# A second layer of 512 rows in seven block products, with its weight scale from squares

## The chip, the cores and the metric

The kernel runs on one core of a Trainium2 chip. The metric is device time in microseconds (us). Before the change the median of three runs is 934.13 us (931.35 to 936.52).

## The reference

Three parts follow one another: a decayed linear attention (4 x 8 heads of 768 steps, 48 wide), a gated dense mixture on its 3072 x 384 output, and a second mixture with eight experts, of which each token takes the best two:

```python
for e in range(E):                       # 8 experts
    for k in range(2):
        mask = top2[:, k] == e
        h = np.maximum(x[mask] @ w1[e], 0.0)                # 384 -> 1024
        out[mask] += top2_w[mask, k, None] * (h @ w2[e])    # 1024 -> 384
```

## The kernel before

Everything in float32 is carried as two float16 halves, high and low; a product A x B is three matmuls, high x high, high x low, low x high, added up in PSUM. `split` cuts a tile: ScalarE copies it to float16 (line 180), VectorE subtracts that copy from it (line 182 or 184).

The change lies in the second mixture (`experts`, line 1107). Each expert has 832 slots for its tokens: part 0 of 512 rows, part 1 of 320, the last 64 of which (`first_few`, `last_few`) are computed only if the expert has more than 768 tokens, inside a branch on the chip. The tokens are gathered by GpSimd's indirect DMAs and turned by SP's transposing DMAs.

- First layer (`layer1`): for each of eight blocks of 128 hidden units, 9 matmuls of 512 or 256 columns fill one PSUM bank (there are eight); ScalarE takes the relu as high half, VectorE relu minus high half as low half.
- Second layer (`layer2`): for each tile of 128 rows, 24 matmuls of 384 columns, hidden blocks as stationary operand; ScalarE scales the result by each row's gate (`put`) and GpSimd adds it to the output in memory by an indirect DMA.
- Weights of the expert after next (`weight_steps`) are fetched in halves on SP's queue into three float32 buffers, `greatest` finds the largest magnitude, `over_all` spreads it over partitions by a one-column matmul, `scales` makes powers of two of it, `cut_up` splits. These steps stand in the list `todo`, and `prepare(n)` issues the next n of them, behind the last VectorE and ScalarE instruction issued so far.

The order of an expert e is: first layer of part 0 (eight blocks, in the first two of which the short rest of expert e-1 is finished), the short rest's first layer, first layer of part 1, four second-layer tiles of part 0, two of part 1. TensorE's order is as written; each engine works through its instructions in one fixed order.

Of the kernel before, what the change touches and what calls it, by code (L numbers as in the profile page):

```python
# [78 lines left out]


@with_exitstack
def body(ctx, tc, q, k, v, alpha, mw1, mw2, mw3, mwo, wg, wn, noise, ew1, ew2, out, dbg=None):
# [39 lines left out]
    wp = ph1.enter_context(tc.tile_pool(name="wp", bufs=1))  # L122
    xp = ph1.enter_context(tc.tile_pool(name="xp", bufs=3))
    sp = ph1.enter_context(tc.tile_pool(name="sp", bufs=2))
    gp = ph1.enter_context(tc.tile_pool(name="gp", bufs=2))
    ps = ph1.enter_context(tc.tile_pool(name="ps1", bufs=8, space=PSUM))
# [711 lines left out]
    ep = None  # L838
# [26 lines left out]
    def weight_steps(src, e, n, m, hi, lo, sc):  # L865
# [25 lines left out]
        def scales():  # L891

            nc.vector.tensor_copy(sc[:, 1:2], s["pm"])
            nc.vector.tensor_scalar(sci[:, 2:3], sci[:, 1:2], 0x7F800000, None, op0=OP.bitwise_and)
            nc.vector.tensor_scalar(sci[:, 2:3], sci[:, 2:3], float(64 << 23), None, op0=OP.max)
            nc.vector.tensor_scalar(sci[:, 3:4], sci[:, 2:3], -1.0, float(258 << 23), op0=OP.mult, op1=OP.add)
            nc.vector.tensor_scalar(sci[:, 4:5], sci[:, 2:3], -float(4 << 23), None, op0=OP.add)
# [5 lines left out]

        return ([lambda i=i: get(i) for i in range(2)] + [lambda i=i: greatest(i) for i in range(2)] +
# [48 lines left out]
    def put(py, n, mt, wv, t, e=None):  # L953
        ys = ep.tile([P, DM], F32, name="ysb", bufs=3)
        nc.scalar.activation(ys[:n], py, AF.Copy, scale=wv[:n, t:t + 1])  # L955

        def add():
# [25 lines left out]
    EW, EX, EH, WV = {}, {}, {}, {}  # L983
# [60 lines left out]

    def second(e, p, t, midway=None):
# [45 lines left out]

    def next_weights(e):
        a, b = weights_for(e)
        todo.extend(pause(1) + a[2:4] + pause(1) + a[5:10] + b[1:2] + a[10:] + pause(1) + b[2:4] + pause(2) + b[5:])
# [12 lines left out]
    def experts():  # L1107
# [5 lines left out]
        rank(NG - 1)  # L1113
        rb = ep.tile([P, E], BF, name="rb", bufs=1)
# [30 lines left out]
        for e in range(1, E):  # L1145
            if e > 1:
                for f in range(NF):
                    first(e, 0, f)
# [24 lines left out]
            for t in range(NTP[0]):  # L1173
                second(e, 0, t)
                prepare(2)
                if e + 1 < E:
                    turn_part(e + 1, 0, t)
            prepare(len(todo))
            if e + 2 < E:
                next_weights(e + 2)  # L1180
            if e < E - 1:
                for t in range(NTP[1] - 1):
                    turn_part(e + 1, 1, t)
                    py = cleared(NK) if t else None
                    second(e, 1, t)
                turn_part(e + 1, 1, NTP[1] - 1)
# [4 lines left out]
        return li  # L1191

# [103 lines left out]
    overflow(li)  # L1296
    ph1.close()
# [31 lines left out]
```

## Time and profile before

| what | value |
|---|---|
| median of 3 runs | 934.13 us |
| profiled execution | 934.74 us, span 933.0 us |
| TensorE busy | 898.9 us, 96% |
| VectorE, ScalarE, GpSimd busy | 67%, 48%, 28% |
| granted TensorE clock, mean | 0.986 |

The span is the profiled execution without what lies around it (1.74 us). Matmuls overlap, so their pace is read from the distance of their starts and not from a row's length. The profile calls TensorE PE (its weight loads PEld), VectorE DVE, ScalarE ACT, GpSimd POOL and SyncE SP.

### The profile page before, as it was taken

What the parts mean: (1) busy time and instruction counts of PE and PEld (TensorE: products, weight loads), DVE (VectorE), ACT (ScalarE), POOL (GpSimd) and SP (SyncE); (2) the same over time, 40 slices, a digit from 0 to 9 for tenths busy, and PEclk for the clock granted to TensorE, in tenths of its full rate; (3) what the DMA queues carried; (4) which work ended last, traced back from release to release, by engine and by line L of the source; (5) the groups of instructions that cost most, each with busy time, mean ns of one, the idle gap of its engine ahead of it and who ended that gap; (6) DMA issues with size and microseconds to landing.
All of it is one profiled execution on the core that took longest, in us unless ns stands there. A gap on an engine that the chain in (4) does not pass through costs nothing. (4 is left out here: it accounts for less than half of the span.)

```text
span 933.0 us, 17675 instructions
## 1 busy us (share of the span) xinstructions
PE 898.9 (96%) x6824; PEld 600.8 (64%) x6824; DVE 624.3 (67%) x1733; ACT 448.2 (48%) x916; POOL 258.3 (28%) x246
## 2 busy tenths in 40 slices
PE   8779999999999999999999999999999999999997
PEld 4667777777767666576665555865656565657574
DVE  7998878488779789597768874556455555555320
ACT  2576766364475654755546534334343443434321
POOL 2311110003041131514132234442333333343203
PEclk9889899999999999999999999999999999999999
DMA  9889582241504435101129248495768677776304
GB/s 244 230 150 148 143 199 76 35 94 49 122 10 104 68 95 77 44 26 42 63 69 195 94 77 205 79 221 95 190 118 182 130 163 148 154 156 137 39 10 48
DMA packets 189274, 105.63 MB, mean 113 GB/s; under 512 B 156912, under 2 KB 174912, under 8 KB 189184
## 3 DMA queue, kind: packets, MB, share of 16 engines
q1 hardware_dynamic: 172624, 68.04, 33.8%
q0 software_dynamic: 16560, 36.37, 18.2%
q8 instruction: 59, 0.97, 0.4%
q14 instruction: 31, 0.25, 0.1%
HBM read 73.06 MB, written 20.31 MB: 100 GB/s over the span
## 5 line engine op out<-in xcount | busy, mean ns | idle before, releaser
L958 POOL DMA_INDIRECT out_dram<-ysb,mt x56 | 88.3, 1578 | 145.0 <-ACT ysb L955 138.0
L922 PE MATMUL ps<-xT,eh 128*128 128x256 f16 (+1 forms) x384 | 125.0, 326 | 1.8 <-DVE hl L926 0.6
L934 PE MATMUL ps<-eh,hl 128*128 128x384 f16 x384 | 125.2, 326 | 0.0
L933 PE MATMUL ps<-el,hh 128*128 128x384 f16 x384 | 125.2, 326 | 0.0
L932 PE MATMUL ps<-eh,hh 128*128 128x384 f16 x384 | 125.1, 326 | 0.0
L924 PE MATMUL ps<-xT,el 128*128 128x256 f16 (+1 forms) x384 | 125.1, 326 | 0.0
L923 PE MATMUL ps<-xT,eh 128*128 128x256 f16 (+1 forms) x384 | 125.1, 326 | 0.0
L926 DVE SCALAR_TENSOR_TENSOR hl<-ps,hh 128x512 f16<-128x512 f32 (+1 forms) x128 | 69.6, 554 | 79.4 <-ACT hh L925 75.3
L925 ACT ACTIVATE hh<-ps 128x512 f16<-128x512 f32 (+1 forms) x128 | 62.3, 489 | 79.5 <-PE ps L924 65.9
L955 ACT ACTIVATE ysb<-ps,wv 128x384 f32<-128x384 f32 (+1 forms) x56 | 32.4, 579 | 136.5 <-PE ps L934 67.9
L700 POOL DMA_INDIRECT table<-md,ad x48 | 51.3, 1069 | 155.4 <-DVE ad L697 103.7
L184 DVE SCALAR_TENSOR_TENSOR el<-es,esc,eh 128x512 f16<-128x512 f32 (+1 forms) x80 | 66.9, 853 | 35.2 <-ACT eh L180 34.9
L545 ACT ACTIVATE ab<-ps 128x384 f32<-128x384 f32 (+2 forms) x136 | 63.1, 471 | 39.4 <-PE ps L543 24.1
L910 POOL DMA_INDIRECT xg<-x2s,mt x56 | 54.4, 971 | 99.7 <-DMA mt<-table 64.7
L182 POOL TENSOR_TENSOR sm<-sf,sm 128x512 f16<-128x512 f32 x24 | 30.0, 1278 | 153.9 <-ACT sm L180 153.9
L541 PE MATMUL ps<-xT,w0h 128*128 128x384 f16 (+2 forms) x204 | 65.0, 320 | 0.9 <-ACT xT L408 0.9
L541 PE MATMUL ps<-xT,w1h 128*128 128x384 f16 (+2 forms) x204 | 65.1, 320 | 0.8 <-DVE Kt L246 0.4
L570 PE MATMUL ps<-Wh,gh 128*128 128x400 f16 x192 | 63.9, 333 | 1.8 <-ACT gh L180 1.5
L542 PE MATMUL ps<-xT,w1h 128*128 128x384 f16 (+2 forms) x204 | 65.1, 320 | 0.0
L543 PE MATMUL ps<-xT,w0l 128*128 128x384 f16 (+2 forms) x204 | 65.0, 320 | 0.0
L542 PE MATMUL ps<-xT,w0h 128*128 128x384 f16 (+2 forms) x204 | 65.0, 320 | 0.0
L543 PE MATMUL ps<-xT,w1l 128*128 128x384 f16 (+2 forms) x204 | 65.0, 319 | 0.0
(303 smaller groups left out, 2085.5 us busy)
## 6 DMA issues: line engine op xcount, KB each, us to landing
es<-in_moe_w_dram SPq DMA_DIRECT2D x32, 768.0 KB
s<-in_moe_w_dram POOLq DMA_DIRECT2D x16, 512.0 KB
out_dram<-zero POOLq DMA_DIRECT2D x5, 960.0 KB
v<-in_v_dram SPq DMA_DIRECT2D x24, 192.0 KB
x2s<-xr SPq DMA_DIRECT2D x24, 192.0 KB
pad<-in_alpha_dram SPq DMA_DIRECT2D x21, 192.0 KB
pad<-in_q_dram SPq DMA_DIRECT2D x21, 192.0 KB
pad<-in_k_dram SPq DMA_DIRECT2D x21, 192.0 KB
```

Source lines behind the costliest of these rows:

```text
L184: nc.vector.scalar_tensor_tensor(lo, src, scale, hi, op0=OP.mult, op1=OP.subtract)
L541: nc.tensor.matmul(pm, wab[i][0][:, kk, fs], xT[:, kk, cs], start=kk == 0, stop=False)
L542: nc.tensor.matmul(pm, wab[i][0][:, kk, fs], xT[:, NK + kk, cs], start=False, stop=False)
L543: nc.tensor.matmul(pm, wab[i][1][:, kk, fs], xT[:, kk, cs], start=False, stop=kk == NK - 1)
L922: nc.tensor.matmul(pm, w1h[:, kk, fs], xT[:, kk, :n], start=kk == 0, stop=False)
L923: nc.tensor.matmul(pm, w1h[:, kk, fs], xT[:, NK + kk, :n], start=False, stop=False)
L924: nc.tensor.matmul(pm, w1l[:, kk, fs], xT[:, kk, :n], start=False, stop=kk == NK - 1)
L926: nc.vector.scalar_tensor_tensor(hl[:, f], pm, 0.0, hh[:, f], op0=OP.max, op1=OP.subtract)
L932: nc.tensor.matmul(py[:n], hh[:, f, ts], w2h[:, f], start=f == 0, stop=False)
L933: nc.tensor.matmul(py[:n], hh[:, f, ts], w2l[:, f], start=False, stop=False)
L934: nc.tensor.matmul(py[:n], hl[:, f, ts], w2h[:, f], start=False, stop=f == NF - 1)
L958: i = nc.gpsimd.indirect_dma_start(out=out, out_offset=bass.IndirectOffsetOnAxis(ap=mt[:n, t, 0:1].bitcast(U32), axis=0), in_=ys[:n], in_o ...
```

## The change

For experts 2 to 7 the second layer of part 0, (512 x 1024) x (1024 x 384), is cut into 2 x 2 blocks (256 rows, 512 hidden units, 192 columns) and done in seven block products, in Winograd's form of Strassen's scheme. Left operands are blocks of the hidden tile, or sums of them; right operands are blocks of the second weights, or differences of them.

- `first_pair` replaces `first` there: blocks come in pairs (f, f + 4), and after the second of a pair VectorE forms four sums, and six of the seven left operands are split from float32.
- The weight list of these experts grows by `diffs` and four `pairs`: four differences of weight blocks and their halves.
- `second_pair` does the products for two tiles of 128 rows each; some products add into a bank that has been read before. Results are scaled into `yq` by ScalarE, or scaled and added by VectorE; four sends go out in the last two products.
- For all experts `greatest` is a square with a running sum on ScalarE, written over the place of the high half, and `scales` works from the mean square.
- The order of the weight steps is new: two steps after each product and after each second-layer tile of part 1, the first fetch after the third product, the next two after the last.

```diff
         def greatest(i):
-            nc.vector.tensor_reduce(sc[:, 5 + i:6 + i], s[i], AX.XY, OP.max, apply_absolute_value=True)
+            nc.scalar.activation(half(hi, i), s[i], AF.Square, accum_out=sc[:, 5 + i:6 + i])
             if i:
                 s["m"] = ep.tile([P, 1], BF, name="em")
-                nc.vector.tensor_reduce(s["m"], sc[:, 5:7], AX.X, OP.max)
+                nc.vector.tensor_tensor(s["m"], sc[:, 5:6], sc[:, 6:7], OP.add)
...
+        def differ(x):
+
+            t = s["d", x] = qp.tile([P, HT, HD], F32, name="td", bufs=3)
+            a, b = ((block(0, 1), block(0, 0)), (block(1, 1), s.get(("d", 0))),
+                    (block(1, 0), s.get(("d", 1))), (block(0, 1), block(1, 1)))[x]
+            nc.vector.tensor_tensor(t, a, b, OP.subtract)
+
+        def cut_diff(x):
+            split(s["d", x], ET[e][0][:, x], ET[e][1][:, x], sc[:, 3:4])
+
+        def diffs():
+
+            ET[e] = [qp.tile([P, 4, HT, HD], F16, name=f"t{y}") for y in "hl"]
+            differ(0)
+            differ(1)
+
+        def pairs(x):
+            cut_diff(x)
+            if x < 2:
+                differ(x + 2)
...
+    def first_pair(e, i):
+
+        f = i // 2 + i % 2 * HT
...
+        if i % 2 == 0:
+            u = qp.tile([P, 6, HP], F32, name="u", bufs=3)
+            nc.scalar.activation(u[:, 0], pm[:, 0], AF.Relu)
+            V.scalar_tensor_tensor(u[:, 5], pm[:, 1], 0.0, u[:, 0], op0=OP.max, op1=OP.subtract)
+            EH[e, "u"] = (u, pm)
+            return
+        u, p0 = EH.pop((e, "u"))
+        nc.scalar.activation(u[:, 1], pm[:, 1], AF.Relu)
+        V.scalar_tensor_tensor(u[:, 2], p0[:, 1], 0.0, u[:, 1], op0=OP.max, op1=OP.add)
+        V.tensor_tensor(u[:, 3], u[:, 2], u[:, 0], OP.subtract)
+        V.scalar_tensor_tensor(u[:, 4], pm[:, 0], 0.0, u[:, 3], op0=OP.max, op1=OP.subtract)
+        nc.scalar.activation(bh[:, 2, j], pm[:, 0], AF.Relu)
+        V.scalar_tensor_tensor(bl[:, 2, j], pm[:, 0], 0.0, bh[:, 2, j], op0=OP.max, op1=OP.subtract)
+        split(u[:, :4], ah[:, :, j], al[:, :, j])
+        split(u[:, 4:], bh[:, :2, j], bl[:, :2, j])
...
+        sums = ((X, 0, plain(0, 0)), (Z, 6, plain(1, 0)), (X, 3, diff(1)), (Y, 2, diff(0)), (X, 5, diff(3)),
+                (Y, 4, plain(1, 1)), (X, 1, diff(2)))
+        after = ((0, 0, False), (0, 0, True), (0, 1, False), (1, 1, False), (1, 1, True), (0, 1, True), (1, 0, False))
+        for m, ((bk, x, (rh, rl)), (r, c, add)) in enumerate(zip(sums, after)):
+            lh, ll = left(x)
+            for k in range(n):
...
+                for f in range(HT):
+                    nc.tensor.matmul(bk[k], lh[:, f, ts], rh[:, f], start=new and f == 0, stop=False,
+                                     skip_group_check=True)
+                    nc.tensor.matmul(bk[k], lh[:, f, ts], rl[:, f], start=False, stop=False, skip_group_check=True)
+                    nc.tensor.matmul(bk[k], ll[:, f, ts], rh[:, f], start=False, stop=f == HT - 1,
+                                     skip_group_check=True)
...
+                if add:
+                    nc.vector.scalar_tensor_tensor(o, bk[k], wv[:, t:t + 1], o, op0=OP.mult, op1=OP.add)
+                else:
+                    nc.scalar.activation(o, bk[k], AF.Copy, scale=wv[:, t:t + 1])
+                if m >= len(sums) - 2:
+                    send(ys[k][r], P, mt, t, e)
+            between(m)
...
+    def next_pair(e, a, b):
+        a[1]()
+        b[0]()
+        todo.extend(a[2:3] + pause(3) + a[3:4] + pause(1) + a[5:10] + b[1:2] + a[10:] + b[2:3] + pause(5) +
+                    b[3:4] + pause(1) + b[5:])
...
+    def between(e, m):
+        prepare(2)
+        if m == 2 and e + 2 < E:
+            EW["next"] = open_weights(e + 2)
+        if e + 1 < E and 2 <= m < 2 + NTP[0]:
+            turn_part(e + 1, 0, m - 2)
```

## Rows read from the trace of the kernel before

**Rows 1.** The page's first part: engine, busy us, share of the span, instructions.

```profile
PE 898.9 (96%) x6824; PEld 600.8 (64%) x6824; DVE 624.3 (67%) x1733; ACT 448.2 (48%) x916; POOL 258.3 (28%) x246
```

**Rows 2.** Windows: start:end and length, then busy us of each engine, clock, DMA.

```profile
500.00:550.00 50.00, 48.16 (x274) 25.89 (x273) 43.67 (x165) 27.20 (x56) 7.50 (x8) 1.00 0.52 114
679.00:727.00 48.00, 47.70 (x296) 28.41 (x294) 25.93 (x47) 19.20 (x35) 17.55 (x14) 1.00 0.76 152
```

**Rows 3.** Waits of TensorE from 500 us on: total us, times, longest.

```profile
PE ps L889 <- DVE em L884: 1.1, 1, 1.1
```

**Rows 4.** Timeline of TensorE and its weight loads: start, us, engine, line, operation.

```profile
631.54 0.19 PE L946 MATMUL ps<-hh,eh 128*128 128x64 f16 x1
...
679.21 0.38 PE L922 MATMUL ps<-xT,eh 128*128 128x512 f16 x1
...
695.75 0.27 PE L922 MATMUL ps<-xT,eh 128*128 128x256 f16 x1
...
703.60 0.33 PE L932 MATMUL ps<-eh,hh 128*128 128x384 f16 x1
...
711.43 0.32 PE L932 MATMUL ps<-eh,hh 128*128 128x384 f16 x1
...
727.03 0.38 PE L922 MATMUL ps<-xT,eh 128*128 128x512 f16 x1
...
838.90 0.19 PE L1036 MATMUL ps<-xT,eh 128*128 128x64 f16 x1
...
919.71 0.19 PE L946 MATMUL ps<-hh,eh 128*128 128x64 f16 x1
919.71 0.10 PEld L947 LDWEIGHTS <-el 128*128 128x128 f16 x1
...
919.74 0.10 PEld L948 LDWEIGHTS <-eh 128*128 128x128 f16 x1
...
921.81 0.33 PE L932 MATMUL ps<-eh,hh 128*128 128x384 f16 x1
```

**Rows 5.** Timeline of VectorE in expert 2's first layers.

```profile
645.35 0.15 DVE L894 TENSOR_SCALAR esc<-esc 128x1 int32<-128x1 int32 x1
645.54 0.15 DVE L895 TENSOR_SCALAR esc<-esc 128x1 int32<-128x1 int32 x1
...
650.40 0.42 DVE L926 SCALAR_TENSOR_TENSOR hl<-ps,hh 128x256 f16<-128x256 f32 x1
650.73 0.75 DVE L184 SCALAR_TENSOR_TENSOR el<-es,esc,eh 128x512 f16<-128x512 f32 x1
```

**Rows 6.** Groups by line in 679 to 727 us, then two of the whole span.

```profile
L958 POOL DMA_INDIRECT out_dram<-ysb,mt x7 | 10.8, 1548 | 13.5 <-ACT ysb L955 13.2 <-issue 0.3
...
L881 DVE TENSOR_REDUCE esc<-es 128x1 f32<-128x1536 f32 x4 | 7.0, 1744 | 0.0
...
L926 DVE SCALAR_TENSOR_TENSOR hl<-ps,hh 128x512 f16<-128x512 f32 x8 | 5.5, 689 | 10.6 <-ACT hh L925 9.3 <-issue 1.3
...
L180 ACT ACTIVATE eh<-es,esc 128x768 f16<-128x768 f32 x4 | 3.5, 924 | 0.0
L955 ACT ACTIVATE ysb<-ps,wv 128x384 f32<-128x384 f32 x6 | 3.5, 581 | 16.9 <-issue 6.9 <-PE ps L934 6.1 <-PE ps L889 3.9
L926 DVE SCALAR_TENSOR_TENSOR hl<-ps,hh 128x256 f16<-128x256 f32 x8 | 3.3, 418 | 0.2 <-ACT hh L925 0.2
L925 ACT ACTIVATE hh<-ps 128x256 f16<-128x256 f32 x8 | 3.1, 385 | 1.5 <-PE ps L924 1.5
...
L182 DVE TENSOR_TENSOR gl<-ab,gh 128x384 f16<-128x384 f32 x60 | 34.0, 566 | 14.9 <-ACT gh L180 13.6 <-issue 1.2
L180 ACT ACTIVATE sm<-sf 128x512 f16<-128x512 f32 x24 | 14.9, 630 | 17.3 <-DVE sf L306 16.0 <-issue 1.1
```

**Rows 7.** Single lines: engine, operation, count, duration ns min/median/max.

```profile
L950 ACT ACTIVATE yt<-ps x8: 325/331/331, 597.4 to 922.0; 128x192 f32<-128x192 f32 x8
...
L575 ACT ACTIVATION_READ_ACCUMULATOR xr<-ps x24: 188/194/215, 173.6 to 528.9; 128x1 f32 x24
```

More of the change, by code (lines that the diff above doesn't have):

```diff
@@ L78 @@
 SX2 = SW * SW * SG * SW
+NQ = 2
+HP = G0 // 2
+HT = NF // 2
+HD = DM // 2
 @with_exitstack
@@ L121, in body @@
     ph1 = ExitStack()
[L122 to L123 removed]
+    ps = ph1.enter_context(tc.tile_pool(name="ps1", bufs=8, space=PSUM))
     sp = ph1.enter_context(tc.tile_pool(name="sp", bufs=2))
[L125 to L126 removed]
+    mixing = ExitStack()
+    wp = mixing.enter_context(tc.tile_pool(name="wp", bufs=1))
+    xp = mixing.enter_context(tc.tile_pool(name="xp", bufs=3))
+    gp = mixing.enter_context(tc.tile_pool(name="gp", bufs=2))
     stg_ = ExitStack()
@@ L902, in cut_up, with block, paired, weight_list @@
             split(x[:, r], h[:, r], l[:, r], sc[:, 3:4])
+        def block(i, c):
+            return s[i][:, :, c * HD:(c + 1) * HD]
+        def differ(x):
[13 more added lines that the diff above has]
+                differ(x + 2)
+        if n == NF and paired(e):
+            return weight_list(get, greatest, over_all, scales, cut_up, n) + [diffs] + [
+                lambda x=x: pairs(x) for x in range(4)]
+        return weight_list(get, greatest, over_all, scales, cut_up, n)
+    def paired(e):
+        return isinstance(e, int) and e >= NQ
+    def weight_list(get, greatest, over_all, scales, cut_up, n):
         return ([lambda i=i: get(i) for i in range(2)] + [lambda i=i: greatest(i) for i in range(2)] +
@@ L1043, in first_few @@
         nc.vector.scalar_tensor_tensor(hl, pm, 0.0, hh, op0=OP.max, op1=OP.subtract)
+    def first_pair(e, i):
+        f = i // 2 + i % 2 * HT
+        if i == 0:
+            EH[e, 0] = [ep.tile([P, NF, G0], F16, name=f"h{x}0", bufs=1).rearrange(
+                "p f n -> p (f n)").rearrange("p (a f n) -> p a f n", a=4, f=HT) for x in "hl"]
+            EH[e, 2] = [qp.tile([P, 3, HT, HP], F16, name=f"h{x}2", bufs=1) for x in "hl"]
+        w1h, w1l, xT = EW[e][0], EW[e][1], EX[e, 0][1]
+        (ah, al), (bh, bl) = EH[e, 0], EH[e, 2]
+        fs, j = slice(f * P, (f + 1) * P), f % HT
+        pm = bank(2, HP)
+        pf = pm.rearrange("p a b -> p (a b)")
+        for kk in range(NK):
+            nc.tensor.matmul(pf, w1h[:, kk, fs], xT[:, kk], start=kk == 0, stop=False)
+            nc.tensor.matmul(pf, w1h[:, kk, fs], xT[:, NK + kk], start=False, stop=False)
+            nc.tensor.matmul(pf, w1l[:, kk, fs], xT[:, kk], start=False, stop=kk == NK - 1)
+        V = nc.vector
+        if i % 2 == 0:
[13 more added lines that the diff above has]
+        split(u[:, 4:], bh[:, :2, j], bl[:, :2, j])
@@ new lines, in second_pair, with left, plain, diff @@
+    def second_pair(e, between):
+        mt = EX[e, 0][0]
+        wv = WV[e, 0] = factors(mt, NTP[0], EW[e][2], EW[e][5], 0)
+        w2, dd = EW[e][3:5], ET.pop(e)
+        a, b = EH[e, 0], EH[e, 2]
+        def left(x):
+            return [h[:, x] if x < 4 else g[:, x - 4] for h, g in zip(a, b)]
+        def plain(i, c):
+            return [w[:, i * HT:(i + 1) * HT, c * HD:(c + 1) * HD] for w in w2]
+        def diff(x):
+            return [d[:, x] for d in dd]
+        n = HP // P
+        X, Y, Z, ys = [], [], [], []
+        sums = ((X, 0, plain(0, 0)), (Z, 6, plain(1, 0)), (X, 3, diff(1)), (Y, 2, diff(0)), (X, 5, diff(3)),
[4 more added lines that the diff above has]
+            for k in range(n):
+                new = len(bk) <= k
+                if new:
+                    bk.append(bank(HD))
+                if m == 0:
+                    ys.append([qp.tile([P, DM], F32, name="yq", bufs=2 * n) for _ in range(2)])
+                ts = slice(k * P, (k + 1) * P)
+                for f in range(HT):
[4 more added lines that the diff above has]
+                                     skip_group_check=True)
+                t = r * n + k
+                o = ys[k][r][:, c * HD:(c + 1) * HD]
+                if add:
[5 more added lines that the diff above has]
+            between(m)
@@ L1113, in experts @@
         rank(NG - 1)
+        nonlocal qp
+        mixing.close()
+        qp = more_room.enter_context(tc.tile_pool(name="qp", bufs=2, reuse_waits="tile"))
         rb = ep.tile([P, E], BF, name="rb", bufs=1)
@@ L1147, in experts @@
                 for f in range(NF):
-                    first(e, 0, f)
+                    if paired(e):
+                        first_pair(e, f)
+                    else:
+                        first(e, 0, f)
                     if f == 0:
@@ L1172, in experts @@
                 fetch_part(e + 1, 1)
[L1173 to L1179, printed above, removed]
+            if paired(e):
+                second_pair(e, lambda m: between(e, m))
+                if e + 2 < E:
+                    next_pair(e + 2, *EW.pop("next"))
+            else:
+                for t in range(NTP[0]):
+                    second(e, 0, t)
+                    prepare(2)
+                    if e + 1 < E:
+                        turn_part(e + 1, 0, t)
+            if e < NQ:
+                prepare(len(todo))
                 next_weights(e + 2)
@@ L1296, in body @@
     overflow(li)
+    more_room.close()
     ph1.close()
```

22 lines of the change are left out of this document (16 added, 6 removed).

## The prediction

> **What bounds the kernel now.** I read the page's first part first: TensorE is busy 898.9 us of 933.0, and no other engine is above 67% [rows 1]. Then one expert of the second mixture by itself, from the start of its first layer to the next one's: expert 3, 679.21 to 727.03, 47.82 us. In a window of that stretch TensorE is busy 47.70 of 48.00 us, VectorE 25.93, ScalarE 19.20 [rows 2]. Last the waits of TensorE from 500 us on, of which the longest is 1.1 us [rows 3]. So in the stage that the change touches TensorE sets the time, whatever is taken from its queue comes off the span, and the others have about half of each expert free. The question is whether they still keep up.
>
> The profiled execution took 934.74 us for its span of 933.0; that is 0.61 above the median of 934.13. Sums below are against 934.74; 0.6 is taken off at the end.
>
> **The products.** TensorE's pace is read from starts, not from the 326 ns of a row. 96 matmuls of 384 columns run from 711.43 to 727.03: 162.5 ns each. 72 of 256 columns from 695.75 to 703.60: 109.0. 72 of 64 columns from 919.71 to 921.81: 29.2 [rows 4]. These lie on one line (0.417 ns a column and 2.5 ns), which gives 82.5 ns for 192 columns and 215.8 for 512. Before, the 512-row second layer is 96 x 162.5 = 15.60 us; after, it is 7 products x 2 row tiles x 4 x 3 = 168 matmuls x 82.5 = 13.86. That is 1.74 us an expert and **10.4 us** for six. TensorE's first layers are as they were.
>
> Each of the 168 also loads weights, and a load's row shows 0.10 us [rows 4], longer than 82.5 ns. But in the 64-column stretch such loads of changing weights start every 29 ns, so they overlap and I charge nothing. The Trainium skill speaks against this ("TensorE: Matmul & The Clock Gate", sections "Back-to-back issue gap" and "LDWEIGHTS"): a stream of load and matmul pairs is set by both, about 81 ns at 128 columns, and a load takes its columns over 1.2 GHz, 107 ns here; by that the products would take an estimated 18.0 us and the change would lose. The trace's 29 ns disagrees with it.
>
> **VectorE and ScalarE, by amount.** A VectorE instruction that needs nothing from the one before starts 0.09 us before that one's end (650.40, 0.42 long, then 650.73); one that does starts 0.04 after it (645.35, 0.15 long, then 645.54) [rows 5]. Neither engine's row for 1024 or 1536 elements exists, so I extend the nearest rows by their slope [rows 6]: a subtraction of 1024 is 0.566 + 640 x 1.04 ns = 1.23 us, of 768 0.97, of 512 0.70, of 256 0.43; ScalarE's copy of 1024 is 0.630 + 512 x 0.82 ns = 1.05, its square of 1536 1.47 and, from another row, 0.19 for reading the sum [rows 7].
> - A pair of first-layer blocks: VectorE had 2 x 0.69 us; now four of 0.42, one of 0.43, 1.23 and 0.70: 4.04. Four pairs: +10.7. ScalarE had 2 x 0.60 (0.385 + 256 x 0.82 ns); now 3 x 0.385 + 1.05 + 0.63 = 2.83: +6.6.
> - Weight differences: VectorE 4 x (0.97 + 1.02) = +8.0 (the 1.02 is the cut of 512 in [rows 5], 0.75, and 256 x 1.04 ns), ScalarE 4 x 0.92 = +3.7.
> - The four reductions of 1.744 [rows 6] leave VectorE (-7.0) and come to ScalarE as 4 x 1.66 (+6.6).
> - Evictions of 192 columns: eight on ScalarE (0.58 - 192 x 0.82 ns = 0.42; without a scale it is 0.33 [rows 7]) and six on VectorE (0.35) for four of 0.58: +1.0 and +2.1.
>
> VectorE 25.9 + 13.8 = 39.7, ScalarE 19.2 + 17.9 = 37.1, of 46.1 us. Both fit, at 86% and 80%. No engine becomes the bound over an expert; the cost is local.
>
> **Where TensorE could wait: the first layer.** A pair on VectorE in its order, start to start: 0.33, 0.46, 0.47 and 0.33 for the four sums, 0.33 for the third low half, 0.45 idle until ScalarE has cut the four sums (it can start only after the third), 1.14, 0.61: 4.12 us. TensorE makes a pair in 18 x 215.8 ns = 3.88. With three cuts of weights (0.66 each), the scales (0.7) and the memset (0.4), VectorE has 19.6 us of work beginning at 2.6, so it ends at 22.3 if pauses are filled with the next block's relu, 24.4 if not; I walked both. TensorE reaches the 256-row layer at 16.54 (695.75 - 679.21) with three of the eight banks still held, and has five. Its eighth block there, at 23.4, wants the bank of the short 64-row rest, whose low half comes after the last pair: free between 23 and 25. That is a wait of 0 to 1.6 us.
>
> The second place is the matmul that spreads the weight scale over partitions. From expert 3 to 6 its second square is queued during the first product and the matmul stands behind the second one, at 24.39 + 24 x 2 x 82.5 ns = 28.35. ScalarE, after the last pair's cut (about 22.5), has the rest's relu 0.5, eight relus 2.3, three cuts 1.9, a square 1.6, two evictions 0.6, that square 1.6: 8.5, so 31.0, and 31.6 if it began at 23.1. The wait, with the first one inside it, is 2.6 to 3.2 us; where ScalarE takes relus of the 256-row layer in its pauses during the pairs (their blocks are ready from 17.5) it is about 1.0. I take 1.5 for experts 3, 4 and 5, nearer the lower end, since ScalarE has pauses enough in this stage now (19.20 busy of 48 us [rows 2]). Expert 6 has its rest's branch taken, 2.10 us (from 838.90), where expert 3's takes some 0.3 (16.54 less 72 x 215.8 ns leaves 1.0 for two branches and three transposes) [rows 4], so 0 to 1.6: I take 0.5. Expert 2 has the previous rest's branch taken (631.54 [rows 4]) and its squares earlier: 0 to 0.5, I take 0. Expert 7 prepares no weights: 0. Sum **5.0 us**, bounds 3.0 and 11.7.
>
> **What I cost at nothing.** (a) Sums shared in a bank: a bank is read after product 1 and written again in product 3, 2.9 us later; ScalarE has nothing else there. The tightest is the last VectorE addition before product 7: due 2.9 us after its product, behind up to two low halves (1.9) and its twin: spare 0.5. If that cover is gone, up to 1 us an expert. (b) The differences: VectorE runs on for some 7 us after the last product; the 256-row second layer (7.83 us, 703.60 to 711.43 [rows 4]) covers it, with only a memset of VectorE in it. (c) SP's queue: the first weight half is issued at product 3 and used 11 us later. The second and third wait for the differences to let go of their buffers, about 5 us into the 256-row second layer; a half of 128 x 1536 x 4 bytes at the window's 152 GB/s [rows 2] is 5.2 us, and the square that wants it stands in ScalarE's queue 5 us later, ahead of relus. So 0 to 1 us an expert, hidden by ScalarE's pauses; I take 0. The transposes that follow in that queue are wanted 20 us later. (d) GpSimd sends four results in the last two products: 4 x 1.55 = 6.2 us [rows 6]; the next is due after the first tile of 3.9 us and four slots remain, so nothing waits, in the last expert too. (e) Experts 0 and 1: squares for reductions in a stretch where VectorE is busy 43.67 of 50 us, ScalarE 27.20, TensorE idle 1.84 [rows 2]. From -1.1 (the wait behind a reduction [rows 3]) to +1; I take 0.
>
> **Sum.** -10.4 + 5.0 = -5.4: 929.3 for the profiled execution, about **929** for the median. With the bounds of the waits: -7.4 to +1.3, so 927 to 935.
>
> **Rivals.**
> 1. *All hidden.* The instruction order fills every pause and the matmul of the scale finds its operand. For it: a seventh of VectorE and a fifth of ScalarE stay free, and the kernel before places such fillers well (a longest wait of 1.1 us [rows 3]). Against it: the 8.5 us behind the last pair hold 3.2 of squares that were not there. 924 us.
> 2. *VectorE paces the first layer, and the kernel is slower.* Place: the four pairs. If pauses are not filled and the second cut makes VectorE wait as the first does (0.45 more a pair, 1.8 an expert), experts 3 to 5 wait 3.2 + 1.8, expert 6 3.4, and 2 and 7 some 1 together: 19.4 us, less 10.4: +9, about 943. For it: 4.12 against 3.88 before any weight work. Against: the overhang has 7.85 us of 256-row layer to be worked off in. It decides from a mean wait of 3.8 us in experts 3 to 6 on (10.4 + 4.7 over four).
> 3. *The products don't shorten.* If a load's 0.10 us set the pace: 168 x 0.10 = 16.8 us against 15.60, +1.2 an expert, +7.2, about 941. Only the load rows' length speaks for it, and the 29 ns between loads against [rows 4]. By the page of the Trainium skill named above it would be heavier still.
>
> **How the numbers follow.** Forecast 0.54, all hidden 0.22, paced by VectorE 0.20, loads 0.04. A measurement of this kernel tells 0.5% (4.7 us) from no change: faster is below 929.5, slower above 938.8. Faster: 0.22 and half of the forecast, 0.27: 0.49. Slower: 0.04 and 0.14 of rival 2, whose lighter forms end inside: 0.18. Same: 0.33. Range 922 to 939: it leaves out some 0.05 below and the heavier part of rivals 2 and 3 above.
>
> **What would show it.** The matmuls of a product start 82 to 83 ns apart and six second layers of 512 rows take 13.9 us plus their waits; 100 ns would be rival 3. Starts of experts 3, 4 and 5 come 47.82 - 1.74 + 1.5 = 47.6 us apart (46.1 in rival 1, 49 and more in rival 2). TensorE's waits name the scale's matmul behind its sum, and relu or low-half readers of a bank late in the 256-row layer. VectorE is busy about 40 us an expert, ScalarE 37. I am wrong if waits stand at other places (within the products, behind a weight transfer), or if the time changes before 600 us.

## The result, and the profile after

The changed kernel takes **938.85 us** (median of 20 runs, 934.52 to 947.07), the kernel before 934.92 (20 runs): a ratio of **1.0052, interval 1.0038 to 1.0066**. It is slower by half a percent; 929.0 was forecast, with 922 to 939 as the range, so the time lies just inside the range, but on the other side of the kernel before. The profiled execution of after took 934.52 us and is the quickest of the 20. It reaches the second layer of expert 0, up to which the change has hardly begun, at 539.18 us; the one of before was there at 543.84 and the seventeen later ones of kernels with the change's squares at 541 to 550. So I compare the two from that point on and don't read the 4.7 us ahead of it as a gain.

The page of after, first part, to be set beside [rows 1]: TensorE has less to do, VectorE and ScalarE more.

```profile
PE 892.1 (96%) x7256; PEld 629.5 (67%) x7256; DVE 677.3 (73%) x1889; ACT 549.1 (59%) x1100; POOL 268.2 (29%) x246
```

Starts of the second layer of expert 0 and of the first layers of experts 1 to 7, from the timeline of TensorE, and the end of expert 7's products:

| | 0 | 1 | 2 | 3 | 4 | 5 | 6 | 7 | end |
|---|---|---|---|---|---|---|---|---|---|
| before | 543.84 | 559.49 | 629.59 | 679.21 | 727.03 | 774.85 | 822.67 | 872.28 | 915.81 |
| after | 539.18 | 559.83 | 629.18 | 682.62 | 731.34 | 778.90 | 825.71 | 873.91 | 915.70 |
| step grows by | | +5.00 | -0.75 | +3.82 | +0.90 | -0.26 | -1.01 | -1.41 | -1.74 |

(A step is the time from one column to the next; the end of before is 900.21 + 15.60.) Expert 7, which prepares no weights, gains the full 1.74 us. Experts 3 to 6 lose 2.64, 1.48, 0.73 and 0.33 of theirs: 5.2 us. Expert 2 loses 5.56, expert 0 five microseconds though it has no products of the new kind at all. The five largest groups of TensorE's waits (engine, operand and line waited at, what released it, us, times, longest), 500 to 930 us, beside [rows 3]:

```profile
PE ps L896 <- DVE em L891: 8.8, 8, 3.3
PE ps L1152 <- DVE hl L966: 0.7, 2, 0.3
PE ps L962 <- PEq L1063: 0.6, 2, 0.3
PE ps L962 <- DVE u L1115: 0.4, 1, 0.4
PE ps L1155 <- DVE hl L188: 0.4, 1, 0.4
```

L896 is the scale's matmul, the one-column matmul that spreads the sum of the squares over the partitions. Two of its eight waits are over 3 us. And the windows with these two, beside two without (busy us and instructions of PE, PEld, DVE, ACT, POOL; granted clock; DMA share; GB/s):

```profile
550.00:600.00 50.00, 46.67 (x412) 30.34 (x411) 18.47 (x48) 20.43 (x38) 19.86 (x18) 0.97 0.58 124
600.00:650.00 50.00, 49.28 (x417) 30.43 (x416) 31.96 (x64) 29.53 (x52) 24.32 (x17) 1.00 0.72 153
650.00:700.00 50.00, 46.28 (x354) 33.06 (x352) 34.67 (x77) 31.38 (x59) 14.74 (x11) 0.97 0.65 134
700.00:750.00 50.00, 47.99 (x382) 34.28 (x380) 39.21 (x80) 36.29 (x69) 19.13 (x14) 1.00 0.75 145
```

In the windows with these waits the granted clock is 0.97. Right behind either wait it is 0.50, which is 1.2 instead of 2.4 GHz:

```profile
554.40:557.40 3.00, 3.00 (x11) 1.48 (x11) 0.82 (x5) 0.00 (x0) 2.00 (x3) 0.50 0.52 116
663.40:666.60 3.20, 3.20 (x23) 3.04 (x21) 1.07 (x6) 0.42 (x1) 1.89 (x2) 0.50 1.22 286
```

After the one of expert 0, 24 matmuls of 384 columns take 5.41 us instead of 3.89; after the one of expert 2, 120 of 192 columns take 11.55 instead of 9.90. So a wait of 3 us costs 4.7 to 5.

**Expert 0.** TensorE, VectorE and SP of after, then VectorE of before:

```profile
554.40 0.16 PE L896 MATMUL ps<-em,part 128*128 128x1 bf16 x1 [3.33 <-DVE em L891]
```

```profile
554.00 0.28 DVE L1019 TENSOR_SCALAR wv<-mt,esc,esc 128x3 f32<-128x3 f32 x1 [4.82 <-DMA mt<-table]
554.20 0.15 DVE L891 TENSOR_TENSOR em<-esc 128x1 bf16<-128x1 f32 x1
```

```profile
552.46 0.34 SPq L1014 DMA_DIRECT2D mt<-table  x1
```

```profile
550.79 1.73 DVE L881 TENSOR_REDUCE esc<-es 128x1 f32<-128x1536 f32 x1
552.56 0.16 DVE L884 TENSOR_REDUCE em<-esc 128x1 bf16<-128x2 f32 x1
...
558.66 0.29 DVE L976 TENSOR_SCALAR wv<-mt,esc,esc 128x3 f32<-128x3 f32 x1 [4.81 <-DMA mt<-table]
```

The same wait of 4.8 us for a table stands in both kernels at VectorE's `factors` of part 1, which multiplies each row's gate from the table by the weights' scales. Before, the maximum `em` was ahead of it in VectorE's queue; now the sum `em` of two numbers, which depends on ScalarE's squares, has slipped behind it, and TensorE waits for `em`.

**Expert 2.** SP, ScalarE and TensorE of after:

```profile
656.90 0.37 SPq L885 DMA_DIRECT2D es<-in_moe_w_dram  x1
```

```profile
661.42 1.48 ACT L888 ACTIVATE eh<-es 128x1536 f16<-128x1536 f32 x1 [0.81 <-DMA es<-in_moe_w_dram]
```

```profile
663.24 0.16 PE L896 MATMUL ps<-em,part 128*128 128x1 bf16 x1 [3.03 <-DVE em L891]
```

The fourth half of the weights (the second half of the second ones) shares a buffer with the first (there are three), so its fetch waits for the last low half of the first, which VectorE finishes late in the longer first layer: 27.7 us after the expert's start, where the fetch of before was issued at 651.50, after 21.9. VectorE, and then both engines in the stretch before (busy us as above):

```profile
655.47 1.41 DVE L190 SCALAR_TENSOR_TENSOR el<-es,esc,eh 128x512 f16<-128x512 f32 x2
```

```profile
651.65:660.61 8.96, 8.56 (x91) 7.95 (x89) 8.96 (x19) 8.95 (x19) 0.00 (x0) 1.00 0.29 85
```

The square of this half waits 0.81 us for the transfer; the sum and the matmul follow. The transfer is the smaller part of the 3.03 us. In the 9 us before, ScalarE has no pause (8.95 of 8.96 us busy): the six cuts of the first weights, the relus and the other square stand ahead. They come late: the first scale's matmul stands at 641.90, 12.7 us after the start of expert 2; in expert 3 it is at 689.48, 6.9 us after the start. The run with the buffer alone (set 5) bears this out: there the fetch is issued at 645.56 without a long wait, and TensorE still waits 2.08 us at this place.

**Behind that fetch.** The same row in expert 3, and GpSimd's first gather, in after and then in before:

```profile
704.58 0.37 SPq L885 DMA_DIRECT2D es<-in_moe_w_dram  x1
705.00 0.97 SPq L1014 DMA_DIRECT2D mt<-table  x2
...
710.15 1.26 POOL L950 DMA_INDIRECT xg<-x2s,mt  x1 [18.63 <-issue]
```

```profile
682.16 0.57 SPq L971 DMA_DIRECT2D mt<-table  x1
699.32 0.37 SPq L878 DMA_DIRECT2D es<-in_moe_w_dram  x1
...
687.95 1.01 POOL L910 DMA_INDIRECT xg<-x2s,mt  x1 [1.60 <-issue]
```

Before, the next expert's table was fetched ahead of the blocked half and four gathers ran early in the first layer; now the tables stand behind it. The first gather comes 19 us later in the expert (27.5 us after its start instead of 8.7), the last three 6 us later, and all seven stand in the products. In this execution nothing waits for them. This place of the gathers becomes the largest term below.

### The profile page after: what moved, and what is told of

Its sections match the earlier page's. It is cut to its first block, busy times and chain, and to the rows that moved or that the text cites. A ratio compares the mean times of both kernels' runs of the same rounds, so it can differ in the third digit from the quotient of the medians.

```text
span 932.8 us, 18985 instructions
## 1 busy us (share of the span) xinstructions
PE 892.1 (96%) x7256; PEld 629.5 (67%) x7256; DVE 677.3 (73%) x1889; ACT 549.1 (59%) x1100; POOL 268.2 (29%) x246
## 5 line engine op out<-in xcount | busy, mean ns | idle before, releaser
L950 POOL DMA_INDIRECT xg<-x2s,mt x56 | 59.2, 1057 | 119.3 <-issue 73.7
L962 PE MATMUL ps<-xT,eh 128*128 128x256 f16 (+1 forms) x240 | 70.5, 294 | 1.5 <-PEq L1063 0.6
L964 PE MATMUL ps<-xT,el 128*128 128x256 f16 (+1 forms) x240 | 70.5, 294 | 0.0
L963 PE MATMUL ps<-xT,eh 128*128 128x256 f16 (+1 forms) x240 | 70.5, 294 | 0.0
L1001 POOL DMA_INDIRECT out_dram<-ysb,mt x32 | 50.9, 1591 | 56.4 <-ACT ysb L995 52.0
L578 PE MATMUL ps<-Wh,gl 128*128 128x400 f16 x192 | 63.9, 333 | 0.2
L577 PE MATMUL ps<-Wl,gh 128*128 128x400 f16 x192 | 63.8, 332 | 0.0
L186 ACT ACTIVATE eh<-es,esc 128x512 f16<-128x512 f32 (+1 forms) x80 | 61.8, 801 | 2.8 <-DVE esc L903 2.8
L972 PE MATMUL ps<-eh,hh 128*128 128x384 f16 x192 | 63.3, 330 | 0.0
L974 PE MATMUL ps<-eh,hl 128*128 128x384 f16 x192 | 63.2, 329 | 0.0
L973 PE MATMUL ps<-el,hh 128*128 128x384 f16 x192 | 63.2, 329 | 0.0
```

The source lines that it names most:

```text
L577: nc.tensor.matmul(pm, gh[:, ts], Wf[1][:, f], start=False, stop=False)
L578: nc.tensor.matmul(pm, gl[:, ts], Wf[0][:, f], start=False, stop=f == NF - 1)
L962: nc.tensor.matmul(pm, w1h[:, kk, fs], xT[:, kk, :n], start=kk == 0, stop=False)
L963: nc.tensor.matmul(pm, w1h[:, kk, fs], xT[:, NK + kk, :n], start=False, stop=False)
L964: nc.tensor.matmul(pm, w1l[:, kk, fs], xT[:, kk, :n], start=False, stop=kk == NK - 1)
L972: nc.tensor.matmul(py[:n], hh[:, f, ts], w2h[:, f], start=f == 0, stop=False)
```

## The experiments

Theory A: single waits at the scale's matmul, made by the order of in-order queues, with the lower clock behind them. Theory B: VectorE and ScalarE are too full. Theory A2, added in set 2: the late tables pile the gathers, the transposes and the next fetch up in the products. Theory R, formed on the way: the ring of three weight buffers (fetch, square, scale, cut, difference, next fetch) holds the time. The sets ran on several chips (2 and 3 on chips of the same number; the chip of the first measurement is not on record). Each set has its own runs of the kernel before; sets 1, 2, 3 and 5 have the changed kernel itself, set 4 does not. Medians, and ratios to before with their intervals (a ratio is not taken from the medians shown and differs from their quotient by up to 0.2%):

| set | kernel | us | ratio |
|---|---|---|---|
| 1 (before 938.31) | changed, again | 959.96 | 1.0239 (1.0202 to 1.0275) |
| | squares only | 939.87 | 1.0018 (1.0003 to 1.0033) |
| | products only | 963.27 | 1.0266 (1.0238 to 1.0293) |
| | factors late | 955.60 | 1.0196 (1.0158 to 1.0233) |
| 2 (937.73) | changed | 958.82 | 1.0217 (1.0186 to 1.0248) |
| | table first | 944.32 | 1.0076 (1.0046 to 1.0107) |
| | scale later | 953.73 | 1.0160 (1.0129 to 1.0190) |
| | both | 938.76 | 1.0014 (0.9990 to 1.0037) |
| 3 (938.14) | changed | 966.42 | 1.0303 (1.0278 to 1.0329) |
| | all steps | 952.53 | 1.0142 (1.0115 to 1.0170) |
| | weights after products | 964.23 | 1.0286 (1.0256 to 1.0317) |
| 4 (933.92) | base | 935.46 | 0.9997 (0.9975 to 1.0019) |
| | fourth buffer | 928.65 | 0.9946 (0.9922 to 0.9970) |
| | fourth buffer, later | 926.80 | 0.9929 (0.9906 to 0.9952) |
| | no low halves | 934.86 | 1.0014 (0.9989 to 1.0040) |
| 5 (937.30) | changed | 960.39 | 1.0243 (1.0215 to 1.0271) |
| | buffer alone | 943.62 | 1.0071 (1.0044 to 1.0098) |
| | best | 939.56 | 1.0027 (0.9998 to 1.0056) |

### Set 1: the two halves of the change, and expert 0

The changed kernel again.

> The changed kernel as it is, for the median on this chip and for a second profile. Both theories: 0.3 to 0.7% slower than before. Theory A (single long waits of TensorE for the scale's matmul, each followed by a stretch at the lower clock): the profile shows again one wait of over 2 us at line 896 near 551 us and one in expert 2, and what makes this run slower or faster than the first profile (934.5 us) stands at that line or in the clock. Theory B (VectorE and ScalarE too full, many short waits): the difference is spread over experts 2 to 6.

It was 21 us slower than in the first measurement, while the kernel before was 3.4 slower: 2.4% above before, where both theories had 0.3 to 0.7. The waits in experts 0 and 2 are there (3.4 and 3.2 us), and something new: TensorE stands still inside the fifth product of experts 3 to 6. TensorE and then ScalarE in expert 4:

```profile
776.77 0.25 PE L1154 MATMUL ps<-tl,hh 128*128 128x192 f16 x1
777.88 0.25 PE L1155 MATMUL ps<-th,hl 128*128 128x192 f16 x1 [0.86 <-issue]
...
779.30 0.24 PE L1152 MATMUL ps<-th,hh 128*128 128x192 f16 x1 [0.92 <-issue]
```

```profile
779.33 0.42 ACT L1162 ACTIVATE yq<-ps,wv 128x192 f32<-128x192 f32 x1 [3.84 <-remote]
```

"issue" and "remote" mean that no instruction in the profile released them; both engines go on in the same 0.03 us, and the gathers of that expert are issued from 769.17 to 777.07. Behind these gaps the granted clock is 0.50 as well (779.9 to 783.3 us). The execution of the first measurement has none of this.

Squares only (the kernel before with `greatest` and `scales` of the change):

> The kernel before with the squares alone (ScalarE squares for VectorE's reductions, scales from them; no block products). Theory A: VectorE's relief ahead of 545 us gives about 3 us, and the sum of the two halves comes later than VectorE's factors for expert 0's part 1, which wait for a transfer, so TensorE waits about 3 us at line 889 near 551 us: within 2 us of the kernel before. Theory B: nothing is lost there, 1 to 3 us faster than before.

```profile
562.61 0.29 DVE L976 TENSOR_SCALAR wv<-mt,esc,esc 128x3 f32<-128x3 f32 x1 [4.99 <-DMA mt<-table]
562.81 0.15 DVE L884 TENSOR_TENSOR em<-esc 128x1 bf16<-128x1 f32 x1
```

The squares alone bring the order of expert 0, a wait of 3.5 us, and 0.2% (0.0 to 0.3), inside theory A's 2 us. The step of expert 0 grows by 5.35 us and the later ones stay as before, so part of it must be given back ahead of that step; without a profile of before on this chip that is not shown. No wait of TensorE is named issue here.

Products only (the change with the old reductions on VectorE):

> The changed kernel with the reductions back on VectorE (block products alone). VectorE then has about 46 of 46 us an expert. Theory A: no 3 us wait near 555 us, but the early gain is gone too; experts 3 to 6 pay for VectorE's load: 930 to 936 us. Theory B: VectorE paces experts 2 to 6, 2 us or more each: 938 to 948 us, slower than the changed kernel.

Four reductions more for VectorE, and the scale's matmul waits 23.3 us in eight waits between 500 and 950 us; expert 0 has no such wait and its step is that of before (15.65 us). Theory A's 930 to 936 us was missed. That the run is slower than the changed kernel is as theory B said, though 3.3 us is hardly clear of the noise; the step of expert 2 grows from 53.6 to 58.2 us. The moves of the change belong together.

Factors late, the edit for expert 0 alone (in outline):

```
 if t == 0:
+    # behind the last VectorE instruction issued so far, for expert 0, part 1
+    with tc.issue_after(last VectorE instruction):
         WV[e, p] = factors(mt, ...)
```

> The changed kernel; expert 0's factors of part 1 (a VectorE instruction that waits for the table's transfer) are only issued behind the VectorE work that stands ahead of it in the program. Theory A: the wait of 3.3 us at line 896 near 551 us goes to under 0.5, and with it some 1.5 us of low clock: 4 to 5 us below the changed kernel, level with the kernel before. Theory B: under 1 us.

4.4 us less than the changed kernel, as theory A said. The intervals of the two ratios overlap, but the trace is plain: the step of expert 0 falls from 20.84 to 15.65 us, that of before, and 550 to 600 us is back at a clock of 1.00. It is not level with the kernel before; the gaps are still there.

### Set 2: the tables, and the scale's matmul

The changed kernel, as control.

> The changed kernel as it is, as the control of the three runs beside it. Theory A (single waits at the matmul of the scale in experts 0 and 2, each with a lower clock behind it, and gaps in the fifth product) expects those waits of 3 us in experts 0 and 2 again and a time between the two medians seen so far, 939 and 960 us; how much of the difference between these two returns depends on whether the gaps in the fifth product of experts 3 to 6 (about 2 us each in the slower measurement, none in the faster one) are there. Theory B (VectorE and ScalarE too full) has no reason for two so different times of one program.

958.82 us, with the gaps.

Table first: `a[5:10] + b[1:2] + a[10:]` becomes `a[5:11] + b[1:2] + a[11:]`, one step later for the fetch b[1] of the fourth half.

> One edit: for the weights of experts 4 to 7 the fourth half of the weights is fetched one step later, so that on SP's queue it stands behind the token table of the next expert and no longer ahead of it. Theory A2 (pile-up): the fourth half waits for VectorE's low halves until about 22 us into an expert, and all that stands behind it (the tables, so the seven gathers, so the transposes) comes at once with the next weight fetch during the products; completions of the transfers and of TensorE then arrive late and TensorE stands still in the fifth product. It expects the gathers of part 0 some 10 to 15 us earlier, the gaps named issue inside the products gone in experts 3 to 6, and 8 to 15 us less than the control if the control shows them (0 to 2 less if it doesn't). Rival C (the gaps hang on a place of TensorE's or ScalarE's instruction stream, which is the same here): gaps stay, 0 us. Rival B (engines too full): 0 us.

14.5 us less: the largest single term. The first gather of expert 3's stretch comes at 708.24 instead of 717.91, and of the waits named issue one of 0.6 us at the scale's matmul is left within the products. Rivals B and C, with 0 us, are out. Waits of TensorE, 500 to 930 us, of the changed kernel and of this one:

```profile
PE ps L896 <- DVE em L891: 8.8, 6, 3.5
PE ps L1154 <- issue: 3.0, 5, 1.0
PE ps L1155 <- issue: 1.9, 3, 0.9
PE ps L1152 <- issue: 1.8, 5, 0.5
```

```profile
PE ps L896 <- DVE em L891: 9.0, 6, 3.4
...
PE ps L896 <- issue: 0.6, 1, 0.6
```

(A wait counts from the modelled end of the matmul before, so the time lost is more; the steps of experts 3 to 5 fall from 51.46, 53.27 and 50.64 us to 48.31, 47.03 and 47.44.)

Scale later: factors late, and `pause(1)` ahead of the second scale becomes `pause(2)`, in expert 2 `pause(2)` becomes `pause(6)`.

> The waits at the matmul of the scale taken away by order alone: in expert 0 the factors of part 1 are issued only where they are used, as in the run before; in experts 2 to 6 the matmul of the scale of the second weights stands one product later (two more in expert 2), with the steps behind it. Theory A: the wait in expert 0 goes (4.4 us measured for it), that of expert 2 (3.0 to 3.3 us) with the lower clock behind it (1.6 us), and 0.4 us each in experts 3 to 5: 9 to 11 us less than the control. Theory B: the work of VectorE and ScalarE is the same, so waits turn up elsewhere, in the 256-row second layer or the next first layer: 4 us less at most, those of expert 0.

5.1 us less, of which expert 0 is 4.4. Expert 2's wait goes (its step falls from 53.46 to 48.88), but later differences free the buffers later (ScalarE's squares wait 11.8 us for transfers between 680 and 880 us, 8.3 in the control), and the first scale's matmul waits instead: 1.4, 2.0 and 1.6 us in experts 3 to 5. Theory A's 9 to 11 was wrong; theory B's 4 at most is within the noise of it.

Both edits:

> Both edits. Theory A with A2 expects the sum of the two: with gaps in the control 17 to 26 us less than it, without them 9 to 13 less, and in both cases some 8 to 12 us below the kernel before, since then nearly the whole saving of the products (10.4 us) is left. Theory B: within 5 us of the control.

20.1 us less, as the sum had it, but 1.0 us above the kernel before and not 8 to 12 below: that half of theory A's expectation failed. The first scale's matmul waits 2.3 and three times 1.1 us, and 2.8 us of waits named issue now stand outside the products, most of them in short rests' first layers (575 to 578 us and 846 to 849 us), beside gathers.

### Set 3: chasing the wait, and what the gaps need

The changed kernel, as control.

> The changed kernel as it is, control for the two runs beside it. Theory A with A2: the waits of 3 to 3.7 us at the matmul of the scale in experts 0 and 2 are there whatever the chip; the gaps in the fifth product either as in the last two controls (some 2 us an expert, time near 959 us) or absent as in the first measurement (near 939 us).

966.42 us, the slowest of all, with the gaps.

All steps: the first scale one block later as well.

> The two edits together as in the run before (table ahead of the fourth half of the weights; factors of part 1 late in expert 0; matmul of the second scale one product later, three in expert 2), and one more: the matmul of the first scale, which then waited 2.3 us in expert 3 and 1.1 each in experts 4 to 6 for its second square, one block of the first layer later, in expert 2 too (0.4). Theory A: those 6 us go and the lower clock behind the wait in expert 3 (1.7 us), 5 to 8 us less than the run with both edits (which was 0.1% above before): 0.993 to 0.996 of before. Theory B (the engines are full and each wait removed turns up at the next place): no change from it, 1.000 to 1.003.

A miss for both theories: 1.0142, where A had 0.993 to 0.996 and B 1.000 to 1.003. That wait is gone in experts 4 to 6 (2.1 us in expert 3), but the second scale's matmul waits 1.9 to 3.4 us, and a bank 1.6 in each of experts 3 to 5. Only one gap is left (0.5 us, in an earlier stage). Moving waits around gains nothing here.

Weights after products: `if m == 2` becomes `if m == 6` ahead of `open_weights`.

> One edit to the changed kernel: the first half of the next weights is fetched after the last product instead of at the third, behind the four transposes; the gathers and the transposes stay in the products. If the gaps in the fifth product need the weight transfer beside the gathers, they go: 8 to 14 us less than the control, less what a later first square costs (up to 3). If gathers and transposes alone make them, they stay, and the time is that of the control or some us more.

```profile
PE ps L1154 <- issue: 5.9, 6, 1.9
PE ps L1152 <- issue: 2.6, 4, 1.1
```

The gaps stay, so they don't need the weight transfer beside them. They leave the products with the gathers (table first), the transposes being in the products in both.

### Set 4: the ring or VectorE

The base has factors late, table first, and expert 2's own steps moved. No run of the changed kernel stands beside it, so whether it would have had gaps here is not shown.

> The changed kernel with the factors late in expert 0, the table ahead of the fourth half of the weights, and in expert 2 the steps of the first weights two blocks earlier and the matmul of the second scale one product later; experts 3 to 6 keep their places. Theory A (single waits): 9 us less than the run with the table edit alone (1.0076 of before), 4.4 from expert 0 and 4.6 from expert 2 with its lower clock: 0.996 to 1.000. If the waits only move: 1.002 to 1.006.

The number is theory A's, the mechanism is not: expert 2's wait only moved, to the first scale (3.4 us, with the lower clock behind it), and its step is 53.12 us as in the changed kernel. Of the two gains that A added up only expert 0's came; that the ratio came out right is luck.

Fourth buffer (in outline):

```
-s[i] = ep.tile([P, HW], F32, name="es", bufs=3)
+own = second weights, second half, expert 2 and later
+s[i] = qp.tile([P, HW], F32, name="eb", bufs=1) if own else ep.tile([P, HW], F32, name="es", bufs=3)
-u = qp.tile([P, 6, HP], F32, name="u", bufs=3)
+u = qp.tile([P, 6, HP], F32, name="u", bufs=2)
```

> The base, with the fourth half of each expert's weights in a buffer of its own (its room comes from two buffers instead of three for the sums of the first layer), so that its fetch waits for no cut and the second half's fetch for no difference. Theory R (the ring of three buffers holds the time): the squares no longer wait for a transfer, the waits at both matmuls of the scale in experts 3 to 6 (0.6 us each at least) go: 3 to 8 us less than the base. Theory B (VectorE's amount): squares earlier but the low halves not, 0 to 2 us less, or up to 3 more through the missing buffer of the sums.

Fourth buffer, later:

> The run beside it, and the matmul of the second scale one product later in experts 3 to 6 as well. Theory R: with the fourth buffer a later difference no longer delays the next fetch of the second half, so the wait of 1.1 to 2.3 us at the first matmul of the scale that this edit brought before does not come: 1 to 3 us less than the run beside it. Theory B: the later steps of the weights push VectorE's work into the next first layer, 0 to 3 us more.

No low halves:

> The base without the four low halves of the weight differences on VectorE (4 x 1.02 us an expert; the products take a tile of zeros in their place, so that part of the sum is left out). All transfers, ScalarE's steps and TensorE's instructions stay. Theory B: VectorE's queue is shorter by 4 us from the products to the next first layer, and the waits of experts 3 to 6 behind VectorE (scale, u, hl) fall by half or more: 4 to 8 us less than the base. Theory R: the differences themselves free the buffers only 2 to 3 us earlier: 0 to 3 us less.

Steps of experts 3 to 6, from the starts of their first layers: base 49.88, 47.81, 47.66, 48.20 us; fourth buffer 46.65, 46.56, 46.55, 48.20; fourth buffer, later 46.21, 46.26, 46.20, 47.85; no low halves 48.09, 46.67, 46.55, 48.20. With the fourth buffer the waits of these experts at the scale's matmul are down to 0.2 us, ScalarE's squares no longer wait for a transfer (5.6 us in the base between 680 and 820 us), and VectorE is no less busy than in the base (first the base, then the fourth buffer):

```profile
700.00:750.00 50.00, 48.06 (x374) 33.43 (x372) 38.67 (x86) 34.45 (x66) 17.61 (x14) 1.00 0.78 142
```

```profile
700.00:750.00 50.00, 49.36 (x399) 36.01 (x397) 39.95 (x84) 37.37 (x71) 20.62 (x16) 1.00 0.83 153
```

The two runs with the buffer gained 6.8 us and 1.9 more, inside theory R's ranges (the 1.9 is not clear of the noise by itself; the four steps fall by 1.4). So with all of its work VectorE allows steps of 46.6 us, and what held the base there was the ring. That does not make the engines idle: 80% is the mean of 50 us, and in 12 us shortly before the second scale's matmul of expert 3 both are full in the changed kernel of the first measurement:

```profile
699.70:712.00 12.30, 11.41 (x110) 10.06 (x111) 12.06 (x24) 12.30 (x27) 1.55 (x2) 1.00 0.22 65
```

The run without low halves does not tell B and R apart: its median gained 0.6 us, which the noise covers, but the four steps gained 4.0. Those low halves stand between the differences and so in the ring; that this is why is argued, not shown, and 4.0 is also theory B's lower bound. In the mixing stage TensorE waited 1.7 and 1.2 us for VectorE in this run, where the base doesn't:

```profile
PE ps L678 <- DVE M L667: 1.7, 1, 1.7
PE ps L677 <- DVE M L665: 1.2, 1, 1.2
```

### Set 5: the buffer alone, and the version pointed to

The changed kernel, as control.

> The changed kernel as it is, control for the two beside it. As before: waits of 3 to 3.7 us at the matmul of the scale in experts 0 and 2, and, where this chip shows them, gaps of some 2 us in the fifth product of experts 3 to 6; 1.005 to 1.030 of before.

960.39 us, with the gaps.

Buffer alone:

> The changed kernel with one edit: the fourth half of each expert's weights has its own buffer (room from two buffers instead of three for the sums of the first layer). The order of SP's queue stays: the fourth half still stands ahead of the tables. Theory R: its fetch waits for nothing long, so the tables and the gathers behind it come 15 us earlier, the gaps in the products go, and the waits in experts 2 to 6 with them; what is left is expert 0's 4.4 us. 12 to 22 us less than the control if that shows the gaps (959 us or more), 5 to 9 less if not. If the place in SP's queue were what matters and not the buffer, the gathers and gaps would stay: 0 to 4 us less.

16.8 us less with one edit, and of the gaps 0.7 us in three short ones is left. The fetch is issued without a wait and the tables behind it 1.1 us later; the last of the seven gathers is issued at 716.14, ahead of the third product, in the changed kernel beside it at 723.62, where the fifth begins:

```profile
693.87 1.08 SPq L887 DMA_DIRECT2D eb<-in_moe_w_dram  x1
695.01 4.91 SPq L1016 DMA_DIRECT2D mt<-table  x2
```

The waits at the scale's matmul did not go (10.8 us in seven waits, 12.9 in six beside it; 2.1 of 3.0 in expert 2), against theory R's words: its range was met by way of the gaps.

Best:

> The version that the runs point to: the fourth buffer, the factors late in expert 0, the table ahead of the fourth half, the matmul of the second scale one product later (two in expert 2), and the first steps of expert 2's list where the change had them (the move two blocks earlier brought a wait of 3.5 us in the last two runs). Theory R: 2 to 5 us less than the run s3 (0.9929 of before): 0.988 to 0.991.

A miss: 1.0027, not 0.99. Expert 0's and expert 2's long waits at the scale are gone, but on this chip waits named issue come where the gathers now run (1.3 us from 847 to 849 us in expert 6, whose gathers are issued from 839.04 to 847.25; shorter ones in experts 3 to 5), and expert 2 waits 2.2 us once for an eviction. The fastest version against the kernel before is the fourth buffer, later, of set 4, at 0.9929 of before; on a chip that shows the gaps it was not tried.

## Why the prediction was wrong

- **The products: right.** 168 matmuls in 13.86 us (901.84 to 915.70), 82.5 ns each, 1.74 us an expert. The Trainium skill's "TensorE: Matmul & The Clock Gate", section "LDWEIGHTS", gave a load 107 ns, and by that the prediction had an estimated 18.0 us against it. A load's row is 98 ns here, but loads start every 82.5 ns as the matmuls do, so their length does not set the pace.
- **The waits of experts 3 to 6: right in sum, in part by luck**, 5.0 forecast and 5.2 in the execution shown. At the scale's matmuls, forecast with 1.5, 1.5, 1.5 and 0.5 us, TensorE waited 0.2 to 0.6 at a time, which cost 2.8 us from start to start; the other 2.4 are small waits for low halves, three of them inside the products, and for banks, which were taken as nothing. The amounts were a little high: VectorE was busy 36.5 to 36.8 us an expert and ScalarE 32.6 to 34.0, forecast 39.7 and 37.1. (The slopes of 1.04 and 0.82 ns cannot be read off the rows shown in [rows 6], but ScalarE's copies of 1024 and squares of 1536 elements took 1.04 and 1.48 us, where 1.05 and 1.47 had been worked out by them.)
- **"(e) Experts 0 and 1 ... I take 0": wrong, +5.0.** I priced the squares by amount. What they changed was the order: a sum that depends on another engine fell behind a wait for a table that was in the trace of before and cost nothing there. The squares alone bring the wait, and factors late takes it away and gives 4.4 of it back.
- **"Expert 2 ... its squares earlier: 0 to 0.5, I take 0": wrong, +5.6.** The squares stand earlier in the list, but ScalarE comes to them late: the cuts of the first weights stand ahead of them without a pause, which is what I had reckoned with for experts 3 to 6 and not here. That is some 2.2 of the 3.0 us; the other 0.8 is the fetch of the fourth half, which waits for VectorE's low halves. The lower clock behind the wait cost 1.65 us more, which I counted nowhere.
- **"(c) SP's queue ... I take 0": wrong, and in the sets with gaps the largest step.** I followed the second and third half and the transposes, not the fourth half with the tables behind it. Table first is worth 14.5 us where the gaps are, and the buffer that frees the fetch 16.8.
- The sum: -10.4 + 5.2 + 5.0 + 5.6 - 0.75 (expert 1) = +4.6 from the second layer of expert 0 on; the medians differ by 3.9. "Within the products", "behind a weight transfer" and "the time changes before 600 us" were the signs named for being wrong, and all three came.
- Rivals: none as written. VectorE pacing the first layer (943) had the right sign, but not the mechanism: it put 18.4 us into experts 3 to 6, where 5.2 were lost, and nothing into expert 0 and 1 us into experts 2 and 7 together. Loads setting the pace (941) came near the time, but the matmuls start 82.5 ns apart and not 100.

## What to carry to other kernels

When work moves between engines, redo the order of each in-order queue, not only its sum: look in the trace of before for every long wait that costs nothing today, and ask what the change puts behind it. Where a step is added as the last reader of a buffer, follow the ring of that buffer once around, through the queue that issues its next fetch, to all that stands behind that fetch. Read the busy share where the wait ends: here 80% over 50 us hid 12 us in which two engines were full. And a fraction of a percent from one set of runs is not a verdict: here the same change cost 0.5% or 2.2 to 3.0%.

## What was not expected of the hardware

- In sets 1, 2, 3 and 5 TensorE stands still for up to 1.9 us (weights after products) with no releaser in the profile, while or just after GpSimd issues gathers; ScalarE goes on with it, after up to 7.6 us that include its wait for the product. In the first measurement the same program has the gathers in the same products and no such gap. Gathers alone don't bring it: with the squares only, on the chip of set 1, they run in the first layers and TensorE has no such wait. What stops the engines, and why only there, stays open; whether it is the chip or the occasion is not shown. The runs show only that moving the gathers moves or ends it, and that the weight transfer is not needed.
- The two waits of 3 us on TensorE were followed by 1.5 to 1.65 us lost at the lower clock, so each cost half as much again as its length. Some shorter ones were followed by it too (2.3 us in expert 3 of both edits: clock 0.50 from 689.2 to 692.6 us), others not (2.1 us in expert 2 of the buffer alone: 1.00 from 671.2 to 676.0 us).
